# A transformer kernel on one core: any two of three PSUM bank pairs for the attention scores, seven banks in one plan

## The chip, the cores and the metric

The kernel runs on one core of a Trainium2 chip. The metric is the device time of one execution in microseconds (us). Three runs of the kernel before took 1034.35, 1034.98 and 1035.09 us; the median is 1034.98.

## The reference

Two identical layers act on x (2048 tokens, 576 features, bf16). Each layer is an attention block and an MLP block, both with a layer norm in front and a residual:

```
x = x + A(_layernorm(x), wqkv, wo)
x = x + B(_layernorm(x), w1, b1, w2, b2)

A: 32 heads of 18 features; scores q.k * 18**-0.5; query i sees keys i-255 .. i;
   softmax; p.v; times wo (576 x 576)
B: h = gelu(y @ w1 + b1)   (576 -> 4608, tanh form);   h @ w2 + b2   (4608 -> 576)
```

The same weights serve both layers.

## The kernel before

**Chunks.** The 2048 tokens are 16 tiles of 128. Four tiles make a chunk, and the two layers make eight chunks, k = 0 to 7 (`CH`, L308), four for each layer. Attention looks back at most two tiles, so chunk k + 1 can start its attention while chunk k is in its MLP.

**The parts of a chunk.**
- `qkv` (L502): x times wqkv, for each tile six groups of five matmuls with 288 columns (`two_out`, L477; L485 and L491). VectorE copies each group out of PSUM (L513, L521). q and k are then transposed by DMA on SyncE's queue (L528) into `qT` and `kT`.
- `E` (L619): attention, in eight groups of four heads. Each group has three units. A unit is up to 4 x 512 score columns, one PSUM bank for each of the four heads (`scores`, L544; the matmuls in L554). ScalarE takes the exp in two halves of two banks each (L563). GpSimd masks the edge blocks (L584). `pv` (L589) multiplies by v (L601) into one accumulator bank, which VectorE divides out after the third unit (L611, L616). `pT`, which holds the exps, has three slots; `E` adds the PV of a unit after the scores of the two units that follow.
- `tail` (L641): transposes of the attention output (L648), the product with wo (L485, L491 again), the residual (L635), the second layer norm and its transposes (L445).
- `G_part` (L663): mm1, half of the 36 column blocks of w1. For each block f there are five matmuls with 512 columns (L680, L687) and a gelu on ScalarE (L695). A table load on ScalarE stands before (gelu) and after (exp).
- `mm2` (L702): for each tile and each half of the output a group of 18 matmuls with 288 columns (L716), planned in three pieces of six, drained by VectorE (L635, L638).

**The order of the work** is made by a planner (`Plan`, L180) when the kernel is built. Every step is a task with an engine, a cost, a latency and a priority. `schedule` (L226) repeatedly takes the task that can start earliest by these prices; among equals the lowest priority number goes first. The result is a fixed order for each engine; on the chip each engine runs its list in order and waits on semaphores for data and for buffers. `fifo` keeps the tasks of one kind in the order in which they were added. `after` makes a task follow the readers of a buffer in the plan, without adding a wait on the chip.

The main loop (L763) adds, for each k: `E` of k for head groups 0 to 3, mm2 of k - 2 (second half), mm1 of k - 1 (first half), `E` of k for groups 4 to 7, mm2 of k - 1 (first half), qkv of k + 1, the tail of k, and mm1 of k - 1 (second half). What lies between two `E` calls is called a half-chunk below. PE has mm2, qkv and the wo product to fill the time in which the scores wait for the exps; they are called fillers.

**PSUM** has eight banks of 512 fp32 columns. Before the change:
- banks 0 to 3: the scores of a unit, always all four (`psS`, L351), and mm1, by pairs: (0, 1) and (2, 3) in turn (L673). Both name the banks directly, so scores and mm1 follow each other in the order in which they were added.
- bank 4: the accumulator of PV (`B_O`, L352).
- banks 5, 6, 7: the planner's pool (L312). Each filler group takes the bank that has been free longest (L253) and gives it back when VectorE has read it.

A unit's scores therefore wait until both exps of the unit before have read their banks.

Of the kernel before, what the change touches and what calls it, by code (L numbers as in the profile page):

```python
# [170 lines left out]
class Bank:  # L171


    def __init__(self):
        self.no = None
        self.left = 0
        self.free = 0.0


class Plan:  # L180


    def __init__(self, S, pool):
        self.S = S
        self.tasks = []
        self.lw = {}
        self.rd = {}
        self.pool = {b: 0.0 for b in pool}
# [37 lines left out]
    def schedule(self):  # L226
        free = {e: 0.0 for e in ENGS}
        released = {e: [] for e in ENGS}
        for t in self.tasks:
            if t.npred == 0:  # L230
                released[t.eng].append(t)
        bank_free = dict(self.pool)
        order = []
        n = len(self.tasks)
        EPS = 1e-6
        while len(order) < n:
            best = None
            for e in ENGS:
                for t in released[e]:
                    st = max(free[e], t.ready)  # L240
                    if t.alloc:
                        fb = sorted(bank_free.values())
                        if len(fb) < len(t.alloc):
                            continue
                        st = max(st, fb[len(t.alloc) - 1])
                    key = (round(st, 3), t.prio, t.idx)
                    if best is None or key < best[0]:
                        best = (key, t, st)
            assert best is not None, "stuck"
            _, t, st = best  # L250
            released[t.eng].remove(t)
            for h in t.alloc:
                b = min(bank_free, key=lambda x: (bank_free[x], x))  # L253
                h.no = b
                del bank_free[b]
            free[t.eng] = st + t.cost
            t.end = st + t.cost + t.lat
            for h in t.handles:
                h.left -= 1
                h.free = max(h.free, t.end)  # L260
                if h.left == 0:
                    bank_free[h.no] = h.free
            for s, data in t.succ:
                same = s.eng == t.eng == "pe"
                s.ready = max(s.ready, st + t.cost + (t.lat if data and not same else 0.0))
                s.npred -= 1
                if s.npred == 0:
                    released[s.eng].append(s)
            order.append((st, t))
        self.order = order  # L270
        for st, t in order:
            nm = lambda r: f"pb{r.no}" if isinstance(r, Bank) else r
            if t.plain:
                self.S.plain(t.eng, t.fn)
            else:
                self.S.add(t.eng, t.fn, [nm(r) for r in t.reads], [nm(w) for w in t.writes], dma=t.dma, ring=t.ring)
        return max(t.end for t in self.tasks)


PAIR = False  # L280
# [3 lines left out]
def build_kernel(nc, A_x, A_wqkv, A_wo, B_x, B_w1, B_b1, B_w2, B_b2, out):  # L284
# [191 lines left out]

    def two_out(lhs, rhs, n, reads, prio, after=()):  # L477

        bs = [Bank(), Bank()]
        full = slice(0, 128)  # L480
        for o in range(2):
            def fn(e, o=o):
                ins = None
                for c in range(4):
                    ins = e.matmul(bank(bs[o])[:, 0:n], lhs(o, c, full), rhs(o, c, full), start=(c == 0), stop=False)  # L485
# [16 lines left out]
    def qkv(k, i, prio):  # L502
        l, t0, nt = CH[k]
        A = l * NT + t0 + i
        for n, w in enumerate("qkv"):
# [10 lines left out]
            else:  # L516
# [9 lines left out]
                else:  # L526
                    dst, dn = kT[:, :, A % KS, :], f"k{A % KS}"
                add("sp", lambda e, dst=dst, sl=sl: e.dma_start_transpose(dst, qn[:, sl, :]),  # L528
                    reads=[f"qn{sl}h0", f"qn{sl}h1"], writes=[dn], dma="t", ring=8, cost=2.1, lat=1.6, prio=prio)


    def units_of(k):
# [11 lines left out]
    def scores(k, g, parts, prio):  # L544
        l, t0, nt = CH[k]
        T0 = l * NT + t0
        sl = pcount[0] % PS
        pcount[0] += 1

        def fn(e):  # L550
            ins = None
            for (so, qo, nq, col) in parts:
                for j in range(4):
                    ins = e.matmul(psS[:, j, col:col + nq * 128], kT[32 * j:32 * j + 32, g, (T0 + so) % KS, :],  # L554
                                   qT[32 * j:32 * j + 32, g, qo * 128:(qo + nq) * 128], start=True, stop=True, tile_position=(32 * j, 0))
            return ins
        rd = [f"q{qo + i}" for (so, qo, nq, col) in parts for i in range(nq)] + [f"k{(T0 + p[0]) % KS}" for p in parts]
        ncol = sum(p[2] for p in parts) * 128
        add("pe", fn, reads=rd, writes=[f"pb{j}" for j in range(4)], cost=0.06 + ncol * 0.00053, prio=prio, lat=0.15)
        lo = min(p[3] for p in parts)  # L560
        hi = max(p[3] + p[2] * 128 for p in parts)
        for h2 in range(2):
            add("act", lambda e, h2=h2: e.activation(pT[:, sl, 2 * h2:2 * h2 + 2, lo:hi], psS[:, 2 * h2:2 * h2 + 2, lo:hi],  # L563
                                                     ACT.Exp, scale=SCALE),
                reads=[f"pb{2 * h2}", f"pb{2 * h2 + 1}"], writes=[f"p{sl}h{h2}"], cost=0.12 + 2 * (hi - lo) * 0.00083, lat=0.2,
                fifo="act", prio=prio)
        blk = {}
        for (so, qo, nq, col) in parts:
# [94 lines left out]
    def G_part(k, hf, prio):  # L663
# [1 line left out]
        n = nt * 128  # L665
        table("gelu", prio)
        TXm = [f"xm{k % 2}_{i}" for i in range(nt)]
        for pr in range(NFH // 2):
            f0 = hf * NFH + 2 * pr
            B = k * 9 + f0 // 4  # L670
            sl = B % NB1
            pp = (f0 % 4) // 2
            bks = (0, 1) if pr % 2 == 0 else (2, 3)  # L673
            rd = [f"w1a{sl}", f"w1b{sl}_0"] + ([f"w1b{sl}_1"] if PAIR else ["w1Z"]) + TXm
            for o in range(2):
                def fn(e, o=o, sl=sl, pp=pp, bks=bks):
                    ins = None
                    for c in range(4):
                        col = c * 512 + (2 * pp + o) * 128
                        ins = e.matmul(bank(bks[o])[:, 0:n], w1_sb[:, sl, col:col + 128], xnTm[:, k % 2, c, 0:n], start=(c == 0), stop=False)  # L680
                    if PAIR and o == 1:
                        for oo in range(2):
                            ins = e.matmul(bank(bks[oo])[:, 0:n], w1_sb[64 * oo:64 * oo + 64, sl, 2048 + pp * 128:2048 + (pp + 1) * 128],
                                           xnTm[64 * oo:64 * oo + 64, k % 2, 4, 0:n], start=False, stop=True, tile_position=(64 * oo, 0))
                    if not PAIR:
                        col = 2048 + (2 * pp + o) * 128
                        ins = e.matmul(bank(bks[o])[:, 0:n], w1_sb[:, sl, col:col + 128], xnTm[:, k % 2, 4, 0:n], start=False, stop=True)  # L687
                    return ins
                w = [f"pb{bks[0]}", f"pb{bks[1]}"] if (PAIR and o == 1) else [f"pb{bks[o]}"]
                cost = mm_cost(n) * (4 if PAIR else 5) + (mm_cost(n) * 1.2 if PAIR and o == 1 else 0.0)  # L690
                add("pe", fn, reads=rd, writes=w, cost=cost, prio=prio, lat=0.15)
            for o in range(2):
                f = f0 + o
                fl = f - hf * NFH
                add("act", lambda e, f=f, fl=fl, b=bks[o]: e.activation(hT[:, fl, 0:n], bank(b)[:, 0:n], ACT.Gelu_apprx_tanh,  # L695
                                                                       bias=b1col[:, f:f + 1]),
                    reads=[f"pb{bks[o]}", "b1"], writes=[f"h{fl}"], cost=0.2 + n * 0.00087, lat=0.2, fifo="act", prio=prio)
            if f0 % 4 == 2:
# [140 lines left out]
```

## Time and profile before

| what | us |
|---|---|
| median of three runs | 1034.98 |
| profiled execution | 1036.42 |
| its span, first to last instruction | 1034.6 |
| mean granted TensorE clock in it | 0.939 |
| ScalarE: exps (L563), 384 | 351.7 |
| ScalarE: gelus (L695), 288 | 197.9 |
| GpSimd: masks (L584), 368 | 279.2 |
| TensorE: mm2 (L716), 2304 matmuls | 312.5 |
| TensorE: mm1 (L680 and L687), 1440 matmuls | 305.8 + 111.8 |

The last five rows are busy times. Matmuls overlap in the pipeline, so that the busy time of a group is less than its count times the mean duration of one. "PE" is TensorE's matmuls, "PEld" its weight loads, which overlap them; DVE is VectorE, ACT ScalarE, POOL GpSimd, SP SyncE, and "SPq" the DMA queue that SyncE issues to. A wait is named by the line that waited and the line that ended the wait: "PE ps L554 <- ACT pT L563" is a score matmul that waited for an exp.

### The profile page before, as it was taken

The page shows a single profiled execution, that of the slowest core. Times are in us where ns is not written, and L with a number is a line of the kernel's source. Part 1 is how long each engine was busy: PE and PEld are TensorE (multiplying, and loading weights), DVE is VectorE, ACT ScalarE, POOL GpSimd, SP SyncE. Part 2 cuts the span into 40 slices and gives each one's busy share as a digit, 9 for nine tenths or more (in the row PEclk, how much of TensorE's full clock was granted, in tenths as well). Part 3 has the DMA queues.
Part 4 walks back from the last instruction along what each step waited for, and adds up shares of the span by engine and source line. Part 5 has one row for each costly group of instructions (what it writes and reads, how often), then busy time and mean ns, then how long its engine had stood idle before and what let it go on. Part 6 is the DMA issues. An engine that isn't in the chain of part 4 may idle for free.

```text
span 1034.6 us, 22287 instructions
## 1 busy us (share of the span) xinstructions
PE 942.6 (91%) x9312; PEld 585.8 (57%) x9312; DVE 317.0 (31%) x771; ACT 591.9 (57%) x705; POOL 380.3 (37%) x519
## 2 busy tenths in 40 slices
PE   3584789899998999999999999899998979889998
PEld 2352556457574675657565665557565554646566
DVE  4741621154123440244214440242212410132011
ACT  0266466656665676656664666646666566653532
POOL 8344733435142451533232451534233450531000
PEclk9685799799998999999999999999998989979999
DMA  9924311793219632494619432594318732243630
GB/s 250 232 73 64 75 44 50 171 195 113 91 57 184 141 105 92 124 178 99 170 36 231 114 104 93 132 181 110 129 47 190 166 121 93 72 117 99 200 126 24
DMA packets 226756, 126.59 MB, mean 122 GB/s; under 512 B 141792, under 2 KB 226528, under 8 KB 226656
## 3 DMA queue, kind: packets, MB, share of 16 engines
q1 hardware_dynamic: 219456, 122.20, 47.6%
q10 hardware_dynamic: 2432, 2.65, 0.9%
q0 software_dynamic: 4768, 0.31, 0.8%
q8 instruction: 74, 1.21, 0.5%
q14 instruction: 26, 0.21, 0.1%
HBM read 90.10 MB, written 2.36 MB: 89 GB/s over the span
## 4 chain that ended last, share of the span: by engine, by line
PE 81%; POOL 5%; issue 5%; DMA 4%; ACT 2%; DVE 2%; SPq 1%; POOLq 0%; DVEq 0%
PE ps L716 28%; PE ps L680 24%; PE ps L485 10%; PE ps L687 6%; PE ps L601 5%; PE ps L554 5%; POOL pT L584 5%; PE ps L491 2%; DMA attT<-attq 2%; ACT pT L563 2%; DMA xnTa<-xn 2%; DVE st_all L413 1%; DMA hT<-in_A_x_dram 0%; SPq L365 0%; POOL rstd L426 0%
## 5 line engine op out<-in xcount | busy, mean ns | idle before, releaser
L563 ACT ACTIVATE pT<-ps 128x1024 bf16<-128x1024 f32 (+2 forms) x384 | 351.7, 968 | 220.9 <-PE ps L554 220.7
L584 POOL TENSOR_SCALAR_AFFINE_SELECT pT<-pT 128x512 bf16<-128x512 bf16 (+1 forms) x368 | 279.2, 781 | 430.1 <-ACT pT L563 429.9
L716 PE MATMUL ps<-w_sb,hT 128*128 128x288 bf16 x2304 | 312.5, 286 | 0.0
L680 PE MATMUL ps<-xnTm,w_sb 128*128 128x512 bf16 x1152 | 305.8, 389 | 5.6 <-ACT pT L563 5.6
L695 ACT ACTIVATE hT<-ps,b1col 128x512 bf16<-128x512 f32 x288 | 197.9, 687 | 196.7 <-PE ps L687 196.6
L716 PEld LDWEIGHTS ps<-w_sb,hT 128*128 128x128 bf16 x2304 | 212.0, 97 | 70.3 <-issue 17.9
L680 PEld LDWEIGHTS ps<-xnTm,w_sb 128*128 128x128 bf16 x1152 | 112.7, 100 | 137.3 <-issue 12.9
L635 DVE TENSOR_TENSOR x_res<-ps,x_res 128x288 f32<-128x288 f32 x160 | 71.0, 451 | 350.5 <-PE ps L716 308.8
L485 PE MATMUL ps<-wqkv,xnTa 128*128 128x288 bf16 x768 | 130.9, 301 | 20.4 <-DMA xnTa<-xn 20.4
L601 PEld LDWEIGHTS ps<-vA,pT 128*128 128x128 bf16 x2880 | 97.3, 98 | 56.0 <-POOL pT L584 38.1
L601 PE MATMUL ps<-vA,pT 128*128 128x20 bf16 x2880 | 102.1, 173 | 28.6 <-POOL pT L584 28.2
L687 PE MATMUL ps<-xnTm,w_sb 128*128 128x512 bf16 x288 | 111.8, 388 | 0.0
L554 PE MATMUL ps<-qT,kT 32*128 32x384 bf16 (+2 forms) x1408 | 79.2, 294 | 28.6 <-ACT pT L563 27.4
L485 PEld LDWEIGHTS ps<-wqkv,xnTa 128*128 128x128 bf16 x768 | 70.8, 101 | 50.0 <-issue 22.9
L521 DVE CAST qn<-ps 128x288 bf16<-128x288 f32 x128 | 58.1, 456 | 69.4 <-PE ps L491 46.8
L554 PEld LDWEIGHTS ps<-qT,kT 32*128 32x128 bf16 x1408 | 22.7, 94 | 68.1 <-issue 34.2
L611 DVE RECIPROCAL rinv<-ps 128x16 f32<-128x16 f32 x64 | 16.5, 257 | 143.2 <-PE ps L601 143.0
L491 PE MATMUL ps<-wqkv,xnTa 128*128 128x288 bf16 x192 | 57.6, 300 | 0.0
L436 DVE TENSOR_SCALAR xn<-x_res,mv_all,rstd 128x576 bf16<-128x576 f32 x60 | 42.8, 724 | 39.4 <-DMA xnTm<-xn 25.4
L659 POOL TENSOR_TENSOR x_res<-x_res,b2bc 128x576 f32<-128x576 f32 x32 | 44.9, 1402 | 16.1 <-DVE xn L436 16.1
L687 PEld LDWEIGHTS ps<-xnTm,w_sb 128*128 128x128 bf16 x288 | 28.8, 100 | 35.7 <-issue 3.0
L424 POOL TENSOR_SCALAR vtmp<-mv_all 128x1 f32<-128x1 f32 (+1 forms) x43 | 9.3, 216 | 105.4 <-DVE mv_all L415 103.1
(31 smaller groups left out, 347.2 us busy)
## 6 DMA issues: line engine op xcount, KB each, us to landing
w_sb<-in_B_w_dram SPq DMA_DIRECT2D x144, 288.0 KB, 5.3
w_sb<-in_B_w_dram SPq DMA_DIRECT2D x72, 512.0 KB, 3.8
w_sb<-in_B_w_dram SPq DMA_DIRECT2D x72, 64.0 KB, 3.6
hT<-in_A_x_dram SPq DMA_DIRECT2D x4, 576.0 KB, 6.3
out_dram<-xn SPq DMA_DIRECT2D x16, 144.0 KB, 1.8
wqkv<-in_A_wqkv_dram ACTq DMA_DIRECT2D x3, 576.0 KB, 7.5
wo_sb<-in_A_wo_dram ACTq DMA_DIRECT2D x1, 576.0 KB, 9.4
xnTa<-xn SPq DMA_TRANSPOSE x32, 3.3
```

The source lines that it names most:

```text
L485: ins = e.matmul(bank(bs[o])[:, 0:n], lhs(o, c, full), rhs(o, c, full), start=(c == 0), stop=False)
L491: ins = e.matmul(bank(bs[o])[:, 0:n], lhs(o, 4, full), rhs(o, 4, full), start=False, stop=True)
L521: add("dve", lambda e, o=o, b=bs[o], qv=qv: e.tensor_copy(qv[:, o * 16:(o + 1) * 16, 0:DH], bank(b)[:, 0:HB].rearrange("p (h d) -> p h d", ...
L554: ins = e.matmul(psS[:, j, col:col + nq * 128], kT[32 * j:32 * j + 32, g, (T0 + so) % KS, :], qT[32 * j:32 * j + 32, g, qo * 128:(qo + nq) ...
L563: add("act", lambda e, h2=h2: e.activation(pT[:, sl, 2 * h2:2 * h2 + 2, lo:hi], psS[:, 2 * h2:2 * h2 + 2, lo:hi], ACT.Exp, scale=SCALE), r ...
L584: add("pool", lambda e, ap=ap, pat=pat, sgn=sgn, kind=kind: e.affine_select(ap, ap, pattern=pat, compare_op=(ALU.is_ge if kind == "d" else ...
L601: ins = e.matmul(bank(B_O)[:, o:o + VW], pT[:, sl, j, col + qi * 128:col + (qi + 1) * 128], vA[:, (T0 + so) % VS, 4 * g + j, :], start=(fi ...
L635: add("dve", lambda e: e.tensor_tensor(x_res[:, t, sl], bank(b)[:, 0:HB], x_res[:, t, sl], ALU.add), reads=[b], writes=[f"x{t}h{hh}"], cos ...
L680: ins = e.matmul(bank(bks[o])[:, 0:n], w1_sb[:, sl, col:col + 128], xnTm[:, k % 2, c, 0:n], start=(c == 0), stop=False)
L687: ins = e.matmul(bank(bks[o])[:, 0:n], w1_sb[:, sl, col:col + 128], xnTm[:, k % 2, 4, 0:n], start=False, stop=True)
L695: add("act", lambda e, f=f, fl=fl, b=bks[o]: e.activation(hT[:, fl, 0:n], bank(b)[:, 0:n], ACT.Gelu_apprx_tanh, bias=b1col[:, f:f + 1]), r ...
L716: ins = e.matmul(bank(b)[:, 0:HB], hT[:, fl, i * 128:(i + 1) * 128], w2_sb[:, fl, hh * HB:(hh + 1) * HB], start=(fl == 0), stop=(fl == NFH ...
```

## The change

Seven banks are in the plan, 0 to 6, and PV accumulates in bank 7. A `Bank` now has a list of choices and may be a pair of neighbours:

- a filler group (qkv, wo, mm2) takes one of 6, 5, 4;
- an mm1 group takes one of 0, 1, 2, 3, singly, each f by itself;
- a unit's scores take two pairs out of (0, 1), (2, 3), (4, 5), one for each exp.

Of its choices a task takes the one that has been free longest, at a tie the first in the list; a task that needs two pairs can start when both are free. Scores and mm1 keep their order among themselves by `fifo="pa"`. In the plan, scores now follow the PV that last read their `pT` slot, and mm1 of a block follows the mm2 that last read its `hT` block. The planner's price for the q and k transposes goes from 2.1 + 1.6 us to 1.3 + 1.4.

```diff
 class Bank:
-    def __init__(self):
+    def __init__(self, choices, pair=False):
+        self.choices = choices
+        self.pair = pair
...
+    def banks(self):
+        return (self.no, self.no + 1) if self.pair else (self.no,)
...
-        bank_free = dict(self.pool)
+        bank_free = {b: 0.0 for b in range(self.nbanks)}
+
+        def place(t):
+
+            got = []
+            taken = set()
+            when = 0.0
+            for h in t.alloc:
+                best = None
+                for n, c in enumerate(h.choices):
+                    bs = (c, c + 1) if h.pair else (c,)
+                    if any(b in taken or b not in bank_free for b in bs):
+                        continue
+                    key = (max(bank_free[b] for b in bs), n)
+                    if best is None or key < best[0]:
+                        best = (key, c, bs)
+                if best is None:
+                    return None, None
+                got.append(best[1])
+                taken.update(best[2])
+                when = max(when, best[0][0])
+            return got, when
...
-    PL = Plan(S, [5, 6, 7])
+    PL = Plan(S, 7)
...
-    psS = ps[:, 0:2048].rearrange("p (j c) -> p j c", j=4)
-    B_O = 4
+    B_O = 7
+    FILL = (6, 5, 4)
+    MM1 = (0, 1, 2, 3)
+    SC = (0, 2, 4)
+
+    def two(b):
+        return ps[:, b.no * 512:(b.no + 2) * 512].rearrange("p (j c) -> p j c", j=2)
...
-        bs = [Bank(), Bank()]
+        bs = [Bank(FILL), Bank(FILL)]
...
-                    reads=[f"qn{sl}h0", f"qn{sl}h1"], writes=[dn], dma="t", ring=8, cost=2.1, lat=1.6, prio=prio)
+                    reads=[f"qn{sl}h0", f"qn{sl}h1"], writes=[dn], dma="t", ring=8, cost=1.3, lat=1.4, prio=prio)
...
+        bs = [Bank(SC, True), Bank(SC, True)]
...
-                    ins = e.matmul(psS[:, j, col:col + nq * 128], kT[32 * j:32 * j + 32, g, (T0 + so) % KS, :],
+                    ins = e.matmul(two(bs[j // 2])[:, j % 2, col:col + nq * 128], kT[32 * j:32 * j + 32, g, (T0 + so) % KS, :],
...
-        add("pe", fn, reads=rd, writes=[f"pb{j}" for j in range(4)], cost=0.06 + ncol * 0.00053, prio=prio, lat=0.15)
+        add("pe", fn, reads=rd, writes=bs, cost=0.06 + ncol * 0.00053, prio=prio, lat=0.15, alloc=bs, fifo="pa", after=[f"p{sl}h{h}" for h in range(2)] + [f"p{sl}m{m}" for m in range(3)])
...
-                reads=[f"pb{2 * h2}", f"pb{2 * h2 + 1}"], writes=[f"p{sl}h{h2}"], cost=0.12 + 2 * (hi - lo) * 0.00083, lat=0.2,
+                reads=[bs[h2]], writes=[f"p{sl}h{h2}"], cost=0.12 + 2 * (hi - lo) * 0.00083, lat=0.2,
...
-        for pr in range(NFH // 2):
-            f0 = hf * NFH + 2 * pr
...
-            bks = (0, 1) if pr % 2 == 0 else (2, 3)
...
+        for f in range(hf * NFH, (hf + 1) * NFH):
+            sl = (k * 9 + f // 4) % NB1
+            fl = f - hf * NFH
+            bk = Bank(MM1)
...
+            add("pe", fn, reads=[f"w1a{sl}", f"w1b{sl}_0", "w1Z"] + TXm, writes=[bk], cost=mm_cost(n) * 5, prio=prio, lat=0.15, alloc=[bk], fifo="pa",
+                after=[f"h{fl}"])
...
-                b = Bank()
+                b = Bank(FILL)
```

More of the change, by code (lines that the diff above doesn't have):

```diff
@@ L187, in __init__ @@
         self.rd = {}
-        self.pool = {b: 0.0 for b in pool}
+        self.nbanks = nbanks
         self.fifo_last = {}
@@ L240, in schedule @@
                     st = max(free[e], t.ready)
+                    got = ()
                     if t.alloc:
-                        fb = sorted(bank_free.values())
-                        if len(fb) < len(t.alloc):
+                        got, when = place(t)
+                        if got is None:
                             continue
-                        st = max(st, fb[len(t.alloc) - 1])
+                        st = max(st, when)
                     key = (round(st, 3), t.prio, t.idx)
                     if best is None or key < best[0]:
-                        best = (key, t, st)
+                        best = (key, t, st, got)
             assert best is not None, "stuck"
-            _, t, st = best
+            _, t, st, got = best
             released[t.eng].remove(t)
[L252 to L255, printed above, removed]
+            for h, no in zip(t.alloc, got):
+                h.no = no
+                for b in h.banks():
+                    del bank_free[b]
             free[t.eng] = st + t.cost
@@ L261, in schedule @@
                 if h.left == 0:
-                    bank_free[h.no] = h.free
+                    for b in h.banks():
+                        bank_free[b] = h.free
             for s, data in t.succ:
@@ L271, in schedule @@
         for st, t in order:
-            nm = lambda r: f"pb{r.no}" if isinstance(r, Bank) else r
+            names = lambda rs: [n for r in rs for n in ([f"pb{b}" for b in r.banks()] if isinstance(r, Bank) else [r])]
             if t.plain:
@@ L275, in schedule @@
             else:
-                self.S.add(t.eng, t.fn, [nm(r) for r in t.reads], [nm(w) for w in t.writes], dma=t.dma, ring=t.ring)
+                self.S.add(t.eng, t.fn, names(t.reads), names(t.writes), dma=t.dma, ring=t.ring)
         return max(t.end for t in self.tasks)
@@ L667, in G_part @@
         TXm = [f"xm{k % 2}_{i}" for i in range(nt)]
-        for pr in range(NFH // 2):
-            f0 = hf * NFH + 2 * pr
-            B = k * 9 + f0 // 4
-            sl = B % NB1
-            pp = (f0 % 4) // 2
-            bks = (0, 1) if pr % 2 == 0 else (2, 3)
[L674 to L698, printed above, removed]
@@ new lines, in G_part, with fn @@
+        for f in range(hf * NFH, (hf + 1) * NFH):
+            sl = (k * 9 + f // 4) % NB1
+            fl = f - hf * NFH
+            bk = Bank(MM1)
+            def fn(e, f=f, sl=sl, bk=bk):
+                ins = None
+                for c in range(KD):
+                    col = c * 512 + (f % 4) * 128
+                    ins = e.matmul(bank(bk)[:, 0:n], w1_sb[:, sl, col:col + 128], xnTm[:, k % 2, c, 0:n], start=(c == 0), stop=(c == KD - 1))
+                return ins
+            add("pe", fn, reads=[f"w1a{sl}", f"w1b{sl}_0", "w1Z"] + TXm, writes=[bk], cost=mm_cost(n) * 5, prio=prio, lat=0.15, alloc=[bk], fifo="pa",
+                after=[f"h{fl}"])
+            add("act", lambda e, f=f, fl=fl, bk=bk: e.activation(hT[:, fl, 0:n], bank(bk)[:, 0:n], ACT.Gelu_apprx_tanh,
+                                                                bias=b1col[:, f:f + 1]),
+                reads=[bk, "b1"], writes=[f"h{fl}"], cost=0.2 + n * 0.00087, lat=0.2, fifo="act", prio=prio)
+            if f % 4 == 3:
```

5 lines of the change are left out of this document (2 added, 3 removed).

## The prediction

> **What bounds the kernel now.** First the page's first part, for the engine with the most work, then that engine's waits, for what stops it (total us, times, longest).
>
> ```profile
> PE 942.6 (91%) x9312; PEld 585.8 (57%) x9312; DVE 317.0 (31%) x771; ACT 591.9 (57%) x705; POOL 380.3 (37%) x519
> ```
> ```profile
> PE ps L601 <- POOL pT L584: 28.2, 29, 3.1
> PE ps L554 <- ACT pT L563: 27.4, 33, 2.1
> PE ps L485 <- DMA xnTa<-xn: 20.4, 3, 14.8
> ...
> PE ps L680 <- ACT pT L563: 5.6, 8, 1.2
> ```
>
> TensorE (PE) is busy for 942.6 of 1034.6 us, so 92.0 us are open. Of the open time the scores (L554) wait 27.4 us for the exps, PV (L601) 28.2 us for the masks behind the exps, and mm1 (L680) 5.6 us for the exps. The change can reach these three; the 20.4 us of start-up transposes it cannot.
>
> An average hides where this lies, so I cut the span into stages by the windows view (columns: length; busy time of PE, PEld, DVE, ACT, POOL with counts; granted clock; DMA share; GB/s).
>
> ```profile
> 69.68:102.50 32.82, 14.94 (x255) 8.22 (x256) 4.50 (x12) 21.13 (x28) 16.38 (x23) 0.56 0.30 48
> 110.72:141.29 30.57, 22.57 (x334) 15.27 (x334) 17.68 (x41) 20.56 (x22) 22.80 (x30) 0.89 0.22 43
> 186.28:203.40 17.12, 12.21 (x142) 5.79 (x142) 2.09 (x5) 11.66 (x12) 8.58 (x11) 0.60 0.92 210
> 227.30:283.55 56.25, 56.25 (x598) 35.65 (x597) 18.82 (x45) 38.20 (x44) 19.64 (x26) 1.00 0.38 109
> 283.55:306.82 23.27, 23.27 (x301) 16.71 (x303) 4.64 (x11) 15.54 (x16) 9.88 (x14) 1.00 0.09 26
> 306.82:322.80 15.98, 12.99 (x164) 7.30 (x164) 4.29 (x10) 11.66 (x12) 8.58 (x11) 0.79 0.93 222
> 427.54:440.22 12.68, 10.17 (x157) 6.22 (x156) 4.38 (x10) 8.83 (x10) 7.35 (x9) 0.87 0.87 237
> 542.66:552.60 9.94, 9.94 (x132) 7.43 (x133) 5.30 (x12) 6.04 (x9) 5.05 (x8) 1.00 1.23 297
> 658.66:674.40 15.74, 12.75 (x164) 7.18 (x164) 4.38 (x10) 11.61 (x12) 8.58 (x11) 0.78 1.03 224
> 778.41:793.90 15.49, 12.50 (x163) 7.15 (x163) 4.29 (x10) 11.36 (x12) 8.58 (x11) 0.78 0.99 228
> 842.34:858.70 16.36, 9.31 (x130) 4.44 (x131) 1.17 (x3) 11.66 (x12) 8.57 (x11) 0.58 0.49 163
> 899.78:916.80 17.02, 10.06 (x148) 4.92 (x147) 1.17 (x3) 11.89 (x13) 8.58 (x11) 0.60 0.46 149
> ```
>
> There are two kinds. In a first half-chunk (227.30) PE is busy throughout at clock 1.00: nothing to win. At the end of a second half-chunk, from where mm2 runs out (the row 283.55 is still full, 306.82 no longer), PE has holes, and the granted clock falls to 0.58 to 0.87, so that the work between the holes is slow too. The rows 69.68 (chunk 0, nothing to fill with) and 110.72 are of this kind; 542.66 is not.
>
> What sets the pace there is shown by the timeline, once with filler and once without (start, duration; in brackets the idle time before and who ended it).
>
> ```profile
> 294.59 0.40 PE L554 MATMUL ps<-qT,kT 32*128 32x384 bf16 x8
> 294.92 0.91 PE L716 MATMUL ps<-w_sb,hT 128*128 128x288 bf16 x6
> 295.04 1.94 ACT L563 ACTIVATE pT<-ps 128x1024 bf16<-128x1024 f32 x2 [1.11 <-PE ps L554]
> 295.66 0.55 PE L601 MATMUL ps<-vA,pT 128*128 128x20 bf16 x16
> 296.07 1.63 PE L716 MATMUL ps<-w_sb,hT 128*128 128x288 bf16 x12
> 297.63 0.40 PE L554 MATMUL ps<-qT,kT 32*128 32x384 bf16 x8
> 297.74 0.46 DVE L635 TENSOR_TENSOR x_res<-ps,x_res 128x288 f32<-128x288 f32 x1 [0.73 <-PE ps L716]
> ```
> ```profile
> 842.27 0.40 PE L554 MATMUL ps<-qT,kT 32*128 32x384 bf16 x8
> 842.72 1.94 ACT L563 ACTIVATE pT<-ps 128x1024 bf16<-128x1024 f32 x2 [1.10 <-PE ps L554]
> 844.71 0.40 PE L554 MATMUL ps<-qT,kT 32*128 32x256 bf16 x8 [0.72 <-ACT pT L563]
> 845.16 1.94 ACT L563 ACTIVATE pT<-ps 128x1024 bf16<-128x1024 f32 x2 [0.51 <-PE ps L554]
> 847.15 0.61 PE L554 MATMUL ps<-qT,kT 32*128 32x384 bf16 x8
> 847.82 1.94 ACT L563 ACTIVATE pT<-ps 128x1024 bf16<-128x1024 f32 x2 [0.72 <-PE ps L554]
> 851.58 0.60 PE L601 MATMUL ps<-vA,pT 128*128 128x20 bf16 x16 [1.15 <-POOL pT L584]
> 853.14 1.94 ACT L563 ACTIVATE pT<-ps 128x1024 bf16<-128x1024 f32 x2 [0.72 <-PE ps L554]
> 854.31 1.86 PE L680 MATMUL ps<-xnTm,w_sb 128*128 128x512 bf16 x4 [1.22 <-ACT pT L563]
> ```
>
> With filler a unit takes 3.04 us (294.59 to 297.63), all of it PE work; ScalarE (ACT) works 1.94 of it. Without filler it takes 2.44 (842.27 to 844.71, clock still full) and then about 2.66 us, and PE and ACT take turns: since all four banks of a unit must be read before the next unit writes, ACT is idle 0.51 to 0.72 us in each unit while scores are made, and PE is idle while exps run.
>
> **The change part by part.** *Instructions.* None is added or removed: the same matmuls, exps, masks and drains; mm1 is planned by single f and not in pairs, over the same banks 0 to 3. PV's accumulator moves from bank 4 to bank 7 and stays a single bank: nothing. The new planner price of the q and k transposes changes no transpose, only what the planner believes:
>
> ```profile
> 318.48 2.62 SPq L528 DMA_TRANSPOSE qT<-qn  x2
> ```
>
> Two hold SyncE's queue for 2.62 us, 1.31 each, so the new price (1.3) is nearer than the old (2.1). Planned work behind them moves up by tenths of a us; all of mm1's eighteen groups lie between the last scores of a chunk and the first of the next, and hide that. Without this cover it would be 0.8 us for each of the eight transposes of a chunk. I take nothing.
>
> *Third pair, starved units.* Scores can now be written into a free pair and the pair of the first exp while the second exp runs. The cycle is then the exps' 1.94 us plus a small gap (none is in the trace for this case; I take 0.05, from 0 to the 0.51 of now). Five units without filler run from 842.72 to 853.14 + 1.94 = 855.08, 12.36 us; five at 1.99 take 9.95: 2.4 us less. PV doesn't stand in the way if it is ordered behind the next unit's scores; masks fit, as POOL is busy 8.58 us where ACT is 11.66 in the same row.
>
> *Handover to mm1.* Line 680 waited 1.22 us at 854.31 for banks 0 and 1. Now it takes whichever of 0 to 3 is free, and one of three pairs mostly is: 1.2 us less. So a starved stretch gives at least 2.4 + 1.2 = 3.6 us. There are seven (186.28, 306.82, 427.54, 658.66, 778.41, 842.34, 899.78): 25 us.
>
> *At most* such a stretch could shrink to its PE work at full clock, that is length less busy time times clock: 17.12 - 12.21 x 0.60 = 9.8; 5.7; 3.8; 5.8; 5.7; 11.0; 11.0, together 53 us. That needs filler to be left over, because units went faster while there was plenty. There the new rule works against itself: fillers take the bank that has been free longest out of 6, 5, 4, and so hold bank 4 or 5 much of the time, which blocks the third pair. I take two fifths of the way from 25 to 53: 36 us.
>
> *Chunk 0* (69.68:102.50): no filler, so the pair 4-5 is always free. ACT is busy 21.13 of 32.82 us over 14 units; with 14 gaps of 0.05 it would be 21.8, 11.0 less. Scores at half clock take 0.61 us and must fit beside one exp of 0.97 with PV's 0.60: tight, so I take 9, bounds 5.5 (half) to 11.
>
> *Chunk 1, first half* (110.72:141.29): ACT 20.56 of 30.57, at most 10.0 less; but POOL is busy 22.80 there (residual adds between masks) and PE 22.57. I take 4, bounds 2 to 10.
>
> *The new cost.* A filler group now has one to three banks and not always three. When scores hold 4 and 5, the next group waits until bank 6 is drained: in the timeline the group's matmuls give PE free at 297.63 and VectorE's drain ends at 297.74 + 0.46 = 298.20, so 0.57 us if nothing else is ready. Behind this wait on PE's queue stand scores and PV (in the planned order), hence ACT and the masks. Scores too may now wait for a filler's bank, with the fillers queued behind them. Thirteen half-chunks have mm2 as filler beside scores, eight groups each. The lower bound is 0 (scores and PV, 0.33 + 0.41 us of a unit's 3.04, from the starts at 294.59 and 295.66 to the next, fall into the wait); the upper is the rival below. I take one open wait per half-chunk, 13 x 0.57 = 7 us, nearest to the full rows, in which the planner has kept PE at 100% with three banks.
>
> *The sum:* 36 + 9 + 4 - 7 = 42 us. The profiled execution took 1036.4 us (span 1034.6 and 1.8 around it), so 994.4; the median of the runs shown is 1.4 lower (1034.98), so 993 us. At the best ends 53 + 11 + 10 - 0 = 74 less, 961; at the worst 25 + 5.5 + 2 - 30 (four open waits per half-chunk) = 2.5 less, 1032.
>
> **The rivals.** *All holes close.* Scores keep ahead so well that filler never runs out: 53 + 11 + 10 - 7 = 67 less, 968 us. For it: full PE wherever filler exists. Against: fillers sit in the third pair. Chance 0.17.
>
> *PV becomes the wait.* PE is in order. If the plan puts PV of the unit before ahead of the next scores, PE stands at the masks, as at 851.58 (1.15 us), and the scores come late as now; the 28.2 us of L601 against 27.4 of L554 speak for it, the planner's early start for scores against. Only the handover is won, 7 x 1.2 = 8 us: 1027. Chance 0.10.
>
> *Slower: fillers starve on one bank.* If scores hold two pairs throughout and the third turns over at once, fillers have bank 6 alone, and each group waits its 0.57 us: 13 x 8 = 104 mm2 groups, and of 6 x 24 = 144 qkv groups those beside scores, some 132: 236 x 0.57 = 134 us at most. Half covered by scores and PV, 67 us are lost against 49 won: 18 more, 1053. It decides from 49 / 134 = 37% uncovered. The full rows 227.30 and 283.55 would then show holes. Against it: the planner prices drains, and puts whatever starts earliest next. Chance 0.11.
>
> *The clock eats it.* Small waits spread over stretches that are now full: rows with PE busy 80 to 81% of the time had clock 0.78 to 0.87 (306.82, 427.54, 658.66, 778.41), full rows 1.00. If each of the 13 half-chunks lost what the row 306.82 lost to the clock, 12.99 x 0.21 = 2.7 us, and one such dip more for each of the 6 first halves, 19 x 2.7 = 51 less the 7 already counted is 44: 1037. Chance 0.06, half of it slower.
> The Trainium skill (TensorE: Matmul & The Clock Gate, section "A second HAM failure mode: psum-queue depth-cycling") tells of a kernel that cycled through PSUM banks in each iteration, whose PE paused so often between matmul groups that its clock kept dropping to half and recovering; by that rule the time would be 1037, not 993. So far the trace bears it out only in part: the row 227.30 changes banks at every group and stays at 1.00.
>
> *Nothing happens:* the planner finds 4-5 never free. In chunk 0 it is free, so 0.03.
>
> **How the numbers follow.** The forecast, 993, has 0.53. Faster by over 0.2% (about what a measurement of this kernel can tell from no change): 0.53 + 0.17 + 0.10 = 0.80. Within: 0.03 + 0.03 = 0.06. Slower: 0.11 + 0.03 = 0.14. The range takes in 968 and 1027 and most of the forecast's own bounds: 962 to 1030, and leaves out 0.20 above, the rivals from 1035 up.
>
> **What would show it.** Right: at chunk 0's end ACT's idle before an exp falls from 0.5-0.7 to about 0.05, and a unit takes about 2 us; L680's wait for ACT goes; the seven stretches shorten by 3.6 us or more each with a higher clock; L554 <- ACT falls below 10 us; PE's busy time falls a little, by the clock alone. New: waits of L716 or L485 for DVE drains, some 7 us. Wrong: L716 or L485 waiting tens of us for DVE (slower); L601 <- POOL risen over 40 us (PV); full rows with a clock under 1.00.

## The result and the profile after

| | us |
|---|---|
| kernel before, median (1034.35 to 1036.78) | 1035.03 |
| changed kernel, median (1004.27 to 1009.39) | 1005.91 |
| ratio, 95% interval | 0.972, 0.969 to 0.975 |
| forecast, and its range | 993, 962 to 1030 |
| profiled executions, before and after | 1036.42 and 1009.39 |

The change makes the kernel 29 us faster; the forecast was 42. Medians and ratios leave out slow runs (over 1.5% above the fastest of the same kernel): two of the six of the kernel with one filler bank, none elsewhere. The page's first part shows the engine that bounds the kernel, after the change:

```profile
PE 927.4 (92%) x9312; PEld 584.9 (58%) x9312; DVE 311.9 (31%) x771; ACT 586.2 (58%) x705; POOL 378.4 (38%) x519
```

The span fell from 1034.6 to 1007.7 us, by 26.9. PE's busy time fell by 15.2 with the same instructions, while the mean granted clock rose from 0.939 to 0.970. The open time fell by only 11.7, from 92.0 to 80.3. PE's waits say why (line 589 is now the scores, 636 PV, 712 mm1, 737 mm2, 519 qkv and wo; total us, times, longest):

```profile
PE ps L519 <- DMA xnTa<-xn: 25.3, 4, 15.0
PE ps L519 <- DMA attT<-attq: 16.8, 9, 3.6
PE ps L589 <- ACT pT L598: 12.2, 22, 1.3
PE ps L737 <- DVE x_res L670: 5.6, 11, 0.7
PE ps L519 <- DVE qn L555: 4.3, 7, 1.0
PE ps L636 <- POOL pT L619: 3.8, 5, 1.0
```

The waits that the change was forecast to reach did shrink: scores for exps from 27.4 to 12.2 us, PV for masks from 28.2 to 3.8, mm1 for exps from 5.6 to nothing, together 45. Others took their place: wo for the attT transposes rose from 5.4 to 16.8, qkv for xnTa from 20.4 to 25.3, and there are waits of mm2 and qkv for VectorE's drains.

The mechanism itself is seen at the end of chunk 0, where little filler is left. ScalarE's exps before:

```profile
79.94 1.94 ACT L563 ACTIVATE pT<-ps 128x1024 bf16<-128x1024 f32 x2 [0.72 <-PE ps L554]
82.39 1.09 ACT L563 ACTIVATE pT<-ps 128x512 bf16<-128x512 f32 x2 [0.51 <-PE ps L554]
84.09 1.51 ACT L563 ACTIVATE pT<-ps 128x768 bf16<-128x768 f32 x2 [0.61 <-PE ps L554]
86.33 1.94 ACT L563 ACTIVATE pT<-ps 128x1024 bf16<-128x1024 f32 x2 [0.72 <-PE ps L554]
```

After:

```profile
76.72 4.39 ACT L598 ACTIVATE pT<-ps 128x1024 bf16<-128x1024 f32 x6 [0.24 <-PE ps L589]
81.66 4.55 ACT L598 ACTIVATE pT<-ps 128x1024 bf16<-128x1024 f32 x6 [0.55 <-PE ps L589]
86.60 1.94 ACT L598 ACTIVATE pT<-ps 128x1024 bf16<-128x1024 f32 x2 [0.40 <-PE ps L589]
```

The exps of the three units of a head group now run on end, six in 4.39 and 4.55 us, and ScalarE is idle once for a group, 0.40 to 0.55 us, and not before each unit. Three units took 6.39 us before (79.94 to 86.33) and 4.94 after (76.72 to 81.66).

It is also seen beside filler, at the start of the last chunk:

```profile
811.74 1.94 ACT L598 ACTIVATE pT<-ps 128x1024 bf16<-128x1024 f32 x2
...
812.38 0.46 DVE L673 TENSOR_TENSOR xn<-ps,x_res 128x288 bf16<-128x288 f32 x1 [16.21 <-PE ps L737]
...
812.90 0.91 PE L737 MATMUL ps<-w_sb,hT 128*128 128x288 bf16 x6 [0.55 <-DVE xn L673]
...
813.74 0.40 PE L589 MATMUL ps<-qT,kT 32*128 32x384 bf16 x8
...
814.19 3.84 ACT L598 ACTIVATE pT<-ps 128x1024 bf16<-128x1024 f32 x4 [0.51 <-PE ps L589]
...
815.64 0.40 PE L589 MATMUL ps<-qT,kT 32*128 32x256 bf16 x8
```

The row 814.19 has four exps in 3.84 us: the exps of two units run on end, with the scores of the second (815.64) written meanwhile. The row 812.90 is the new cost: mm2 waits 0.55 us for a bank to be drained.

Where the time came from is seen by chunks, each from its first scores to the next chunk's (the last to the end). The profiled execution of the changed kernel is the slowest of its four, 3.5 us above the median, so a difference of 2 or 3 us between chunks should not be leaned on. First before, then after; length, busy times and counts, clock, DMA share, GB/s:

```profile
33.80:99.90 66.10, 37.98 (x537) 23.80 (x536) 25.87 (x71) 36.29 (x48) 32.47 (x46) 0.67 0.51 114
99.90:228.90 129.00, 113.84 (x1116) 67.19 (x1120) 42.61 (x103) 75.82 (x88) 55.13 (x72) 0.88 0.45 104
228.90:349.60 120.70, 117.16 (x1209) 72.80 (x1211) 40.45 (x97) 76.38 (x89) 46.84 (x62) 0.97 0.51 124
349.60:468.70 119.10, 116.00 (x1209) 72.56 (x1208) 40.08 (x97) 76.29 (x89) 47.03 (x62) 0.99 0.51 125
468.70:580.70 112.00, 110.34 (x1045) 69.92 (x1045) 40.26 (x98) 66.14 (x89) 38.56 (x54) 1.00 0.55 134
580.70:700.50 119.80, 116.81 (x1209) 72.94 (x1212) 39.48 (x96) 76.45 (x89) 46.85 (x62) 0.97 0.50 122
700.50:820.60 120.10, 116.81 (x1205) 72.81 (x1204) 34.05 (x82) 76.30 (x89) 45.60 (x60) 0.97 0.53 128
820.60:1034.60 214.00, 196.51 (x1685) 121.28 (x1684) 33.83 (x80) 106.95 (x129) 45.59 (x60) 0.94 0.35 107
```
```profile
34.00:94.20 60.20, 37.37 (x540) 23.73 (x544) 25.63 (x70) 35.82 (x48) 32.17 (x46) 0.72 0.55 132
94.20:212.80 118.60, 107.31 (x1100) 65.12 (x1100) 43.50 (x103) 73.76 (x86) 55.07 (x72) 0.93 0.48 108
212.80:332.70 119.90, 114.71 (x1205) 72.62 (x1204) 39.26 (x97) 75.65 (x88) 46.61 (x62) 1.00 0.55 132
332.70:452.00 119.30, 114.76 (x1209) 72.57 (x1208) 38.87 (x96) 75.65 (x88) 46.61 (x62) 1.00 0.52 125
452.00:570.10 118.10, 113.31 (x1045) 71.02 (x1044) 38.71 (x96) 65.52 (x88) 38.19 (x54) 0.97 0.51 126
570.10:688.80 118.70, 114.76 (x1209) 72.67 (x1209) 38.78 (x96) 75.65 (x88) 46.62 (x62) 1.00 0.51 125
688.80:809.60 120.80, 116.17 (x1205) 73.51 (x1204) 33.16 (x80) 75.65 (x88) 45.48 (x60) 0.99 0.50 122
809.60:1007.70 198.10, 191.84 (x1697) 121.16 (x1696) 33.62 (x80) 107.23 (x130) 45.48 (x60) 1.00 0.39 115
```

Chunk 0 gained 5.9 us, chunk 1 10.4, the last 15.9. The five between lost 5.1 together; chunk 4 alone lost 6.1 (112.0 to 118.1), 3.0 of it in PE's busy time, as the granted clock fell from 1.00 to 0.97. In chunks 2 and 5 PE is busy about 2 us less than before at a clock of 1.00, but is open for 4 to 5 us instead of 3 to 3.5. So the question for the experiments was what kept the gain out of the middle.

### The profile page after: what moved, and what is told of

Same layout as the page of the kernel before. It is cut to its first block, busy times and chain, and to the rows that moved or that the text cites. A ratio compares the mean times of both kernels' runs of the same rounds, so it can differ in the third digit from the quotient of the medians.

```text
span 1007.7 us, 22352 instructions
## 1 busy us (share of the span) xinstructions
PE 927.4 (92%) x9312; PEld 584.9 (58%) x9312; DVE 311.9 (31%) x771; ACT 586.2 (58%) x705; POOL 378.4 (38%) x519
## 4 chain that ended last, share of the span: by engine, by line
PE 68%; DMA 4%; DVE 3%; ACT 3%; issue 1%; POOL 1%; SPq 0%; DVEq 0%
PE ps L737 26%; PE ps L712 24%; PE ps L519 6%; PE ps L636 6%; PE ps L589 4%; DMA attT<-attq 3%; ACT pT L598 2%; PE ps L525 1%; DVE x_res L670 1%; DMA xnTm<-xn 1%; POOL rstd L460 1%; DVE xn L470 1%; ACT hT L716 1%; DVE st_all L447 0%; ACT L753 0%
## 5 line engine op out<-in xcount | busy, mean ns | idle before, releaser
L598 ACT ACTIVATE pT<-ps 128x1024 bf16<-128x1024 f32 (+2 forms) x384 | 347.2, 971 | 133.6 <-PE ps L589 132.2
L712 PE MATMUL ps<-xnTm,w_sb 128*128 128x512 bf16 x1440 | 320.1, 379 | 0.1
L670 DVE TENSOR_TENSOR x_res<-ps,x_res 128x288 f32<-128x288 f32 x160 | 71.0, 450 | 399.9 <-PE ps L737 362.4
L519 PE MATMUL ps<-wqkv,xnTa 128*128 128x288 bf16 x768 | 127.7, 297 | 29.7 <-DMA xnTa<-xn 25.3
L636 PEld LDWEIGHTS ps<-vA,pT 128*128 128x128 bf16 x2880 | 94.4, 96 | 29.1 <-issue 11.2
L519 PEld LDWEIGHTS ps<-wqkv,xnTa 128*128 128x128 bf16 x768 | 73.1, 101 | 58.5 <-issue 18.8
L589 PE MATMUL ps<-qT,kT 32*128 32x384 bf16 (+2 forms) x1408 | 76.5, 285 | 18.7 <-ACT pT L598 12.2
L519 PE MATMUL ps<-wo_sb,attT 128*128 128x288 bf16 x256 | 45.9, 313 | 16.8 <-DMA attT<-attq 16.8
L525 PE MATMUL ps<-wqkv,xnTa 128*128 128x288 bf16 x192 | 56.8, 296 | 0.0
L673 DVE TENSOR_TENSOR xn<-ps,x_res 128x288 bf16<-128x288 f32 x32 | 14.6, 457 | 114.7 <-PE ps L737 114.7
L470 DVE TENSOR_SCALAR xn<-x_res,mv_all,rstd 128x576 bf16<-128x576 f32 x60 | 43.1, 723 | 22.1 <-POOL rstd L460 10.4
L519 PEld LDWEIGHTS ps<-wo_sb,attT 128*128 128x128 bf16 x256 | 26.2, 106 | 30.7 <-DMA attT<-attq 20.6
```

The lines of the kernel that those rows point to most:

```text
L470: add("dve", lambda e: e.tensor_scalar(xn[:, sl, 0:D], s[:, t, :], mv_all[:, t, 0:1], rstd[:, t:t + 1], op0=ALU.subtract, op1=ALU.mult), r ...
L589: ins = e.matmul(two(bs[j // 2])[:, j % 2, col:col + nq * 128], kT[32 * j:32 * j + 32, g, (T0 + so) % KS, :], qT[32 * j:32 * j + 32, g, qo ...
L636: ins = e.matmul(bank(B_O)[:, o:o + VW], pT[:, sl, j, col + qi * 128:col + (qi + 1) * 128], vA[:, (T0 + so) % VS, 4 * g + j, :], start=(fi ...
L670: add("dve", lambda e: e.tensor_tensor(x_res[:, t, sl], bank(b)[:, 0:HB], x_res[:, t, sl], ALU.add), reads=[b], writes=[f"x{t}h{hh}"], cos ...
L712: ins = e.matmul(bank(bk)[:, 0:n], w1_sb[:, sl, col:col + 128], xnTm[:, k % 2, c, 0:n], start=(c == 0), stop=(c == KD - 1))
```

## The experiments

Theory: the third pair alone makes the gain, and part of it is lost again because the plan sends the wo product before its data. Rivals: the gain is the freer mm1 banks or the new price; the loss is a collision of transposes with w2 loads, or nothing that can be filled.

| kernel | median us | ratio to before, 95% interval |
|---|---|---|
| changed | 1005.91 | 0.972 (0.969 to 0.975) |
| changed, two pairs | 1042.95 | 1.008 (1.006 to 1.010) |
| changed, old price, two pairs | 1035.65 | 1.000 (0.998 to 1.001) |
| changed, old price | 1000.15 | 0.966 (0.964 to 0.968) |
| before, new price | 1042.21 | 1.006 (1.004 to 1.008) |
| changed, w2 loads later | 1005.04 | 0.971 (0.969 to 0.974) |
| the same, not in the last chunk | 999.50 | 0.965 (0.962 to 0.967) |
| changed, attT at 4.0 us | 994.55 | 0.962 (0.960 to 0.964) |
| changed, old price and attT at 4.0 us | 993.02 | 0.959 (0.956 to 0.961) |
| changed, nearer latencies for all transposes | 995.23 | 0.961 (0.959 to 0.964) |
| changed, one filler bank | 1127.45 | 1.087 (1.081 to 1.093) |

The kernel before, run beside them, had medians of 1034.69 to 1035.74.

**Without the third pair.**

```diff
-    SC = (0, 2, 4)
+    SC = (0, 2)
```

> The changed kernel with the third pair taken away: scores choose between (0, 1) and (2, 3) only, all else as changed (single mm1 groups, fillers on 6, 5, 4, new transpose price). Theory 'third pair' (the gain comes from scores written while the exps before still run): most of the gain goes, 1022 to 1032 us, and the idle of ACT before an exp in filler-free units is back at 0.5 us or more. Rival 'handover and price' (the gain comes from the freer mm1 banks and the other transpose price): stays at 1000 to 1010 us.

Measured 1042.95 us: not only is the gain gone, the rest of the change costs 8 us. The waits are back: scores for exps 29.2 us, PV for masks 19.7, mm1 for exps 8.0; at the end of chunk 0 ScalarE is again idle 0.51 to 0.72 us before each unit. The theory's number was missed on the slow side; something else in the change loses time.

**The old price.**

```diff
-  ... writes=[dn], dma="t", ring=8, cost=1.3, lat=1.4, prio=prio)
+  ... writes=[dn], dma="t", ring=8, cost=2.1, lat=1.6, prio=prio)
```

> The changed kernel with the old planner price of the q and k transposes (2.1 + 1.6 us in place of 1.3 + 1.4). Theory 'third pair': the price is worth little, 1002 to 1010 us. Rival 'price gave the gain': 1020 us or more. Rival 'price made the plan too hopeful' (it is why PE now waits 16.8 us for attT): the attT wait falls below 8 us and the time to 995 to 1000.

Measured 1000.15: the new price loses 5.8 us, more than the first theory allowed. The attT wait fell to 12.5 us, not below 8, and the xnTa wait to 20.2. The third theory has the direction and, within 0.15 us, its time, but not the whole wait.

**Only the new price, on the kernel before.** The same line, 2.1 + 1.6 replaced by 1.3 + 1.4.

> The kernel before with nothing but the new planner price of the q and k transposes (1.3 + 1.4 us). Theory 'the price costs' (it loses 5 to 6 us with the third pair, by the run with the old price, and is most of the 8 us by which the changed kernel without the third pair is slower than the kernel before): 1038 to 1043 us. Rival 'order rules' (the 8 us come from the rest: mm1 by single blocks, scores after PV and mm1 after mm2 in the plan): 1033 to 1037 us.

Measured 1042.21: 6.7 us lost by the price alone, with attT waits of 10.1 us instead of 5.4.

**Old price and two pairs.** Both edits above in the changed kernel.

> The changed kernel with the old price and without the third pair; what is left of the change is mm1 by single blocks, the order rules of the plan, and the moved PV bank. Theory 'the price costs': like the kernel before or up to 8 us better by the freer handover to mm1, 1027 to 1037 us. Rival 'order rules': 1040 us or more. Against the run with the old price and three pairs it gives the third pair's own worth a second time; 30 to 37 us are expected.

Measured 1035.65, the time of the kernel before. Without the third pair, single mm1 blocks, the order rules and the moved PV bank are together worth nothing; mm1 still waits 5.7 us for exps, so the freer handover needs the third pair too. The four kernels make a square: the third pair is worth 35.5 us at the old price (1035.65 to 1000.15) and 37.0 at the new (1042.95 to 1005.91); the price costs 7.3 without the pair and 5.8 with it. The account of the change closes: about 36 won, 6 to 7 lost, 29 left.

**w2 loads later.**

```diff
-            w2_load(1, b + 3)
+            if last:
+                w2_load(1, b + 3)
...
             tail(k, b + 1.9)
+            if k >= 1:
+                w2_load(1, b + 3, after=[f"aT{i}" for i in range(4)])
```

(`w2_load` hands `after` on to the planner.)

> The changed kernel, with the w2 loads of the second half planned behind the wo product of the tail, so that they are issued after the attT transposes and not before; no wait is added on the chip. Theory 'collision' (scores now end when mm2 ends, so the attT transposes travel together with 2.6 MB of w2 and land late): attT lands in about 3 us instead of 4 to 6, PE's wait for attT falls from 16.8 to under 6 us, and the time to 993 to 999 us. Rival 'chain' (the attT transposes are late because PV, the division and the queue before them are late, whatever else travels): landing and wait stay, 1003 to 1009 us.

Measured 1005.04: no gain, as the rival had it, but PE's wait for attT fell to 4.1 us, as the theory had it. The median time from issue to landing of an attT transpose fell from 3.2 to 2.6 us; it is 2.7 in the run with attT at 4.0 us, which leaves the loads alone, so the median doesn't show a collision. The tail of chunk 4 shows what changed there (start, duration; the SyncE queue's four attT transposes, then PE's first wo matmuls). Changed kernel:

```profile
529.56 6.57 SPq L683 DMA_TRANSPOSE attT<-attq  x4
...
535.48 1.14 PE L519 MATMUL ps<-wo_sb,attT 128*128 128x288 bf16 x4 [3.62 <-DMA attT<-attq]
```

w2 loads later:

```profile
528.25 5.88 SPq L683 DMA_TRANSPOSE attT<-attq  x4
...
532.02 0.67 PE L519 MATMUL ps<-wo_sb,attT 128*128 128x288 bf16 x4 [0.29 <-DMA attT<-attq]
```

From the first issue to the first wo matmul, which needs the first transpose alone, 5.92 us went to 3.77 when w2 didn't travel at the same time; all DMA engines together moved 227 GB/s in the first stretch and 127 in the second. The same holds for chunks 2, 6 and 7, where the first wo matmul came 4.5 to 4.9 us after the issue and now comes after 2.7 to 3.4. In chunks 1, 3 and 5 there is no difference (3.3 to 4.0 us in both). So the collision is real, in four chunks of seven. The last chunk got longer instead, 203.7 us against 198.1; there mm2 waits 3.7 us for w2.

**The same, with the last chunk's loads early.**

```diff
-            if last:
+            if k >= NK - 1:
                 w2_load(1, b + 3)
...
-            if k >= 1:
+            if 1 <= k < NK - 1:
```

> The run with the later w2 loads, but with the loads of the last chunk early as in the changed kernel. Theory 'collision, given back' (later w2 loads do cure the attT wait, and the run showed no gain only because in the last chunk, where no qkv lies between, mm2 then waits for w2): the last chunk, from its first scores to the end, falls from 203.8 us back to about 198, and the time to 996 to 1001 us. Rival 'no collision': 1002 to 1008 us.

Measured 999.50, and the last chunk's row is:

```profile
801.10:998.80 197.70, 191.76 (x1697) 121.07 (x1696) 33.66 (x80) 107.23 (x130) 45.48 (x60) 1.00 0.39 115
```

As the theory had it: moving the loads wins 6 us, which had been given back in the last chunk.

**A nearer latency for attT.**

```diff
-  ... writes=[f"aT{i}"], dma="t", ring=8, cost=1.3, lat=1.4, prio=prio - 0.1)
+  ... writes=[f"aT{i}"], dma="t", ring=8, cost=1.3, lat=4.0, prio=prio - 0.1)
```

> The changed kernel with the planner's latency for the attT transposes at 4.0 us instead of 1.4, which is about what they take; only the order on PE and SP changes. Theory 'order' (the wait for attT is lost because the fixed order puts the wo product in front of mm1 work that is ready): PE's wait for attT falls from 16.8 to under 6 us and the time to 993 to 1000 us. Rival 'nothing to fill with' (at that place no other PE work is ready, so the wait stays or moves to another line): 1002 to 1010 us.

Measured 994.55, 11 us under the changed kernel. The same place in chunk 4:

```profile
526.06 6.89 SPq L683 DMA_TRANSPOSE attT<-attq  x4
...
532.01 0.66 PE L519 MATMUL ps<-wo_sb,attT 128*128 128x288 bf16 x4 [0.62 <-DMA attT<-attq]
```

The transpose takes as long as in the changed kernel (5.95 us), but PE waits 0.62 instead of 3.62: other work was put in front, 5.3 us of qkv matmuls between the issue and the wait instead of 2.3. All waits for attT come to 1.2 us. And the middle chunks now gain most of what the forecast gave them:

```profile
212.60:330.30 117.70, 114.72 (x1209) 72.66 (x1212) 40.23 (x98) 75.66 (x88) 46.74 (x62) 1.00 0.57 136
330.30:448.50 118.20, 114.81 (x1209) 72.62 (x1208) 39.17 (x96) 75.66 (x88) 46.73 (x62) 1.00 0.53 126
448.50:561.90 113.40, 110.61 (x1045) 69.63 (x1044) 39.50 (x96) 65.53 (x88) 38.17 (x54) 1.00 0.53 131
561.90:679.30 117.40, 114.55 (x1209) 72.80 (x1212) 39.08 (x96) 75.65 (x88) 46.73 (x62) 1.00 0.53 127
679.30:796.30 117.00, 114.29 (x1205) 72.80 (x1204) 32.87 (x80) 75.66 (x88) 45.59 (x60) 1.00 0.50 126
```

583.7 us against 591.7 before and 596.8 in the changed kernel.

**Both prices.** The old price for q and k and 4.0 us for attT.

> The changed kernel with the old price for the q and k transposes and the latency of 4.0 us for the attT transposes. Theory 'order' (both prices matter because a hopeful price puts a waiting matmul in front of work that is ready): the two gains of 5.8 and 11 us overlap in part, 987 to 994 us. Rival 'the same hole': both fill the same hole, no better than the better of the two, 994 to 999 us.

Measured 993.02, the lowest of all. Its interval overlaps with that of attT alone, so the two theories aren't told apart by it; with attT priced nearer the q and k price is worth about 1.5 us and not 5.8, which suggests that most of its cost goes through the attT wait.

**Nearer latencies everywhere.** attT 4.0, q and k 3.0, both norm transposes 3.0, each with 1.3 us of the queue.

> The changed kernel with planner latencies near those that the profile of the changed kernel has from issue to landing: attT 4.0 us, q and k 3.0, the two norm transposes 3.0, each with 1.3 us of the queue. Theory 'order' (the plan loses time wherever it believes a transpose lands early): at or under the run with attT alone at 4.0 us, 986 to 994 us, with PE's waits for xnTa, qT and attT together under 25 us. Rival 'only attT matters': 992 to 997 us, waits for xnTa as there (27 us).

Measured 995.23: the theory's time was missed, and the rival's (992 to 997 us) met. The xnTa wait did fall, from 26.9 us with attT alone to 19.8, but qT, kT, attT and the masks took it back (4.0, 2.4, 4.3 and 8.1 us). What a nearer price gives beyond attT isn't settled; the plan is greedy, and any change of it shifts other things.

**One bank for the fillers.**

```diff
-    FILL = (6, 5, 4)
+    FILL = (6,)
```

> The changed kernel with bank 6 as the only bank of the fillers, so that the third pair is always free for scores. It prices the prediction's slower rival. If each filler group then waits 0.57 us with half of it covered, 67 us are lost in the half-chunks with mm2, less what scores gain by the always free pair: 1050 to 1075 us. If scores and PV cover nearly all of it: 1000 to 1015 us. PE's waits of mm2 and qkv for VectorE's drains should rise from 11 us to 50 or more.

Measured 1127.45, 122 us over the changed kernel, beyond the expected 1075. The waits for drains, first four of six:

```profile
PE ps L519 <- DVE qn L555: 44.9, 86, 0.9
PE ps L519 <- DVE vA L547: 19.4, 34, 2.3
...
PE ps L737 <- DVE x_res L670: 13.7, 41, 0.6
PE ps L737 <- DVE xn L673: 9.1, 21, 0.6
```

All waits for drains come to 98 us, against 11 in the changed kernel. qkv waits far more than mm2 (120 waits of 192 groups): a qkv group has five matmuls between two drains, an mm2 group eighteen. The waits are not the whole loss. PE's busy time rose too, from 927.4 to 980.8 us with the same instructions, and the mean granted clock was 0.953, not 0.970. One place where the clock fell is a run of qkv groups, each of which waits 0.55 us at most:

```profile
485.48:494.86 9.38, 5.51 (x36) 2.85 (x36) 3.21 (x7) 0.86 (x1) 0.00 (x0) 1.00 0.63 141
494.86:508.39 13.53, 10.40 (x52) 4.73 (x52) 3.21 (x7) 1.51 (x2) 1.23 (x2) 0.50 0.35 68
```

With the same groups and the same waits the clock is 1.00 in the first row and 0.50 in the second.

## Why the forecast was right, and where its sum was off

**Third pair, starved units: right.** The exps of consecutive units run on end (rows 76.72 and 814.19), with one gap of 0.40 to 0.55 us for three units where 0.05 for each was taken, and PV did not take over as the wait (28.2 to 3.8 us), so that rival is out. Two of the signs named beforehand were missed: scores still wait 12.2 us for exps, not under 10 (8.3 of it before 140 us), and the middle chunks, with four of the seven stretches, got longer. The terms for the pair, the handover and the new stalls came to 42 us; the square gives 35.5 to 37.0.

**The two fifths: right size in places, by luck.** The two stretches of the last chunk were given two fifths of the way from 7 to 22 us, 13; it gained 15.9, stalls included. But fillers in banks 4 and 5 are not what limits it. The scores of the last chunk's first half-chunk now end with its mm2, in a stretch where PE is nearly full:

```profile
809.60:837.70 28.10, 27.15 (x401) 19.19 (x401) 5.73 (x14) 23.26 (x25) 15.57 (x21) 1.00 0.21 65
```

There the limit is PE's own work, not the pair. This is what the rival "all holes close" said, that scores keep ahead so well that filler doesn't run out. Its argument was right here, and the forecast's against it was not. Its time, 968 us, was reached by no run: the last chunk gave 15.9 us of the 22 that such an end was reckoned at.

**Chunk 0:** forecast 9, measured 5.9. **Chunk 1** was given 4 for its first half and, at the same two fifths, 6.1 for the stretch at 186.28: 10.1, measured 10.4. The sum agrees better than its terms: up to the last scores of the first half (99.94 to 139.79 before, 94.17 to 131.39 after) 2.6 us were won, behind it 7.8.

**New stalls: right.** Forecast 13 waits of mm2 for drains, 7 us; measured 11 waits and 5.6 us for L670 in the list above and 2 and 1.1 for L673 beside it, and 0.55 us where 0.57 was worked out. qkv has another 4.3.

**The transposes' price: the step that failed.** The prediction put it: "I take nothing", because mm1 lies between the last scores of a chunk and the first of the next. That covers the transposes themselves. It does not cover what else the planner does with the price: it moves the wo product, behind the same queue, to a place in PE's fixed order where its data isn't there yet. In chunk 4 PE has 2.3 us of other work between the first attT issue and the wait, with the old price 3.5. The price costs 5.8 us with the third pair and 6.7 us on the kernel before alone, nearly half of the distance between 993 and 1005.91; the attT wait is 4.3 and 4.7 us of these. The rest isn't traced. The order shifts elsewhere too: with the old price chunk 0 takes 54.4 us instead of 60.2, and chunk 2 123.2 instead of 119.9.

**Middle chunks: where most of the loss lies.** The four stretches of the middle were to give 17 us, less 6 for stalls; the chunks lost 5.1, and with attT priced nearer they gain 8.0. Their scores did end earlier, but now they end with mm2, while the w2 loads travel and little filler is left. Chunk 4, the end of mm2 and the last scores, before:

```profile
541.02 1.63 PE L716 MATMUL ps<-w_sb,hT 128*128 128x288 bf16 x12
...
550.74 0.29 PE L554 MATMUL ps<-qT,kT 32*128 32x256 bf16 x4
```

After:

```profile
523.90 0.90 PE L737 MATMUL ps<-w_sb,hT 128*128 128x288 bf16 x6
524.73 0.29 PE L589 MATMUL ps<-qT,kT 32*128 32x256 bf16 x4
```

The chain of division, four transposes and wo, which had been under filler, came to the front: 5.4 to 16.8 us of waits. Behind the longest, the 3.62 us in chunk 4, the clock was lower too: 0.54 for 6.5 us, in which four wo matmuls took 1.14 us instead of 0.67 (row 535.48). Two edits that leave the choice of banks alone close the same hole: a nearer latency (wait 1.2 us, time 994.55) and later w2 loads (wait 4.1 us; 3.7 us and 999.50 with the last chunk's loads early). No run gives the nearer latency to the kernel before, whose attT wait is 5.4 us, so how much of the 11 us the banks laid open isn't shown. The forecast asked where a stall goes only for PSUM; it did not ask what stands next on PE once the scores are done.

**The slower rival** did not come true: with three banks to choose from all waits for drains came to 11 us. Its price (67 us lost, 18 net) was too low: with one bank in truth the kernel is 92 us slower than the kernel before, and its clock falls too.

**The clock rival** did not come true either: the chunk row 212.80 has PE open for 5.2 of 119.9 us and a clock of 1.00. The Trainium skill's case of a clock that oscillates under bank cycling (TensorE: Matmul & The Clock Gate, "A second HAM failure mode: psum-queue depth-cycling") doesn't show in the changed kernel; stalls of 0.55 us in an otherwise full stretch (row 809.60) left the clock at full. It does show with one filler bank, where such stalls come at every group (1.00, then 0.50, row 494.86).

## What to carry to other kernels

A third buffer under a two-engine turn (scores, exps) is worth most of the turn's gap in a stretch without filler: in chunk 0 1.4 of the 1.8 us that ScalarE was idle for three units. Where filler keeps the engine full it gains nothing on the spot, but the turn gets ahead, and the filler lasts until the turn is done. When such a stretch ends earlier, look at what stands next in the fixed order and which transfers start at the same moment: here a DMA latency of 1.4 us in the planner, where the reader came 3.3 to 5.9 us after the issue, cost 11 us, nearly a third of what the banks had won. A cheaper price in a planner is an edit of the whole order, and has to be measured alone.

## What the runs showed of the hardware that was not expected

The first attT transpose of chunk 4 was followed by its reader after 5.92 us with w2 loads in flight, and after 3.77 us without. And TensorE's clock falls without any long pause: in the kernel before, the row 842.34 has a granted clock of 0.58 with PE busy 9.31 of 16.36 us, though the longest single PE wait between 825 and 860 us is 1.4 us. With one filler bank it fell to 0.50 in a run of groups that each waited 0.55 us at most, after 9.4 us of the same groups at 1.00; what decides when it falls isn't shown.
